# A Fourier layer with a routed expert on one core: second units, the last eight steps and the drain at the end in another order

## The chip, the core and the metric

One core of a Trainium2 chip runs the kernel. Its engines are TensorE (PE in the profile, with PEld for weight loads), VectorE (DVE), ScalarE (ACT), GpSimd (POOL) and SyncE (SP, which here only issues transfers). The metric is the device time of one execution in microseconds (us).

## What is computed

Eight sequences of 3136 rows and 256 columns go through a Fourier layer and then through an expert that sees only the 128 rows of each sequence with the highest scores:

```python
X = np.fft.rfft(x, axis=1)
Yr = Xr @ w_r - Xi @ w_i + b_r
Yi = Xr @ w_i + Xi @ w_r + b_i
Yr, Yi = soft_threshold(Yr, 0.01), soft_threshold(Yi, 0.01)
y = np.fft.irfft(Yr + 1j * Yi, n=3136, axis=1)
scores = y @ w_gate                        # per sequence b:
top = the 128 rows with the highest score
out[top] = y[top] + sigmoid(scores[top]) * (relu(y[top] @ w1) @ w2)   # 1024 hidden
```

## The kernel before

The transform of length 3136 is split into two stages of 98 and 32, so a sequence passes four matmul stages with transfers through DRAM between them:

- `s1` (L398 on, matmul L405) is the first forward stage, eight **units** a sequence; its result is copied by ACT (`at`) and stored in `As`. `fold` (L394) prepares its input.
- `s2` (L439) is the second forward stage, on `As` loaded as `av`; ACT and DVE split its result into `Xh` and `Xl` (L451, L452). `spectral` (L223 to L225, 18 matmuls, called SPEC below) multiplies with the weights; ACT writes `ks`, POOL `kb`, DVE adds it to `py`; `shrink` makes `Y` (ACT L477, DVE L479).
- `s2i` (L500) is the inverse second stage. Its result lies in the left halves of the PSUM tiles `pca` and `pcb`; ACT copies both (`ct`, L510), DVE reads both for the scores (`junk`, L512, which writes `Csc`), and the copies are stored in `Cs`.
- `s1i` (L568) is the inverse first stage, again eight units a sequence, on `Cs` loaded as `cv` (the loads of C; for the last sequence two of them go into the tiles `xt`). Its result goes through ACT (`ot`, L570) to the output.

`s1` and `s1i` share one PSUM tile, `s`. The same tile takes `spread` (L540), a part of the routing.

**The steps.** There are T = 100 steps t, one for each group (13 groups for an even sequence, one of them shared with the next, 12 for an odd one). A step issues on PE, in this order: `s2` of step t + 1; a first unit of `s1` or `s1i`, if one is due; one turn of the routing; SPEC of step t; pieces of the expert; `s2i` of step t - 1; and then a second unit or a `spread`, if one is due. In 18 steps the second unit is one of `s1i`, in one step at the start one of `s1`. Units fall due at 64 in 100 steps, by `due`.

**The routing** of a sequence (`route`) starts when its last `s2i` is done: `score`, `spread`, eight rounds of `select` that find the score of the 128th row digit by digit (PE sums counts at L239, DVE compares and counts again at L234 to L260), then `place`, which makes the row numbers `idx` (PE L281 to L315). Every round puts small results into the right half of `pca`. A routing is a generator with phases "pe", "da" and "db"; `turn` runs one phase of all of them, so that one step makes one round.

**The expert** of a sequence is `fetch` (an indirect transfer by POOL that collects rows from the output, L330) and then `prepare`, `hidden` (L359), `combine` (L370) and an indirect store (L376). `tick` issues one piece of it. `fetch` needs `idx` and all stores of that sequence's output.

**The end.** After the last step, a loop makes slots: one turn of the routing and `work`, which issues pieces of the expert and left-over units of `s1i` until a load estimate is reached. Before the last `s2i` stands `work(3.6)`. The four loads of C of the last sequence (number 7), 784 KB each, are issued when `rest`, the list of units still to do, has shrunk to 8, 8, 6 and 4.

All engines run the order that the program writes (manual schedule). Transfers issue on SP in program order.

Of the kernel before, what the change touches and what calls it, by code (L numbers as in the profile page):

```python
# [104 lines left out]
def fourier_moe(ctx: ExitStack, tc: tile.TileContext, x, w_r, w_i, b_r, b_i, wg, w1, w2,  # L105
# [121 lines left out]
    def select(b, rep, thrs):  # L227
# [3 lines left out]
        for k, i in enumerate(shifts):  # L231
            c = pool.tile([128, S // 8], BF16, name="c", bufs=1)
            n = pool.tile([128, 1], F32, name="n", bufs=1)
            nc.vector.tensor_scalar(out=c, in0=rep, scalar1=f.bitcast(F32), scalar2=None, op0=ALU.is_ge, op1=ALU.add, accum_out=n)  # L234
            if k > 0 and i > 0:
                nc.vector.tensor_tensor(out=g, in0=digits[:, k + 1:k + 2], in1=w, op=ALU.bitwise_xor)  # L236
# [97 lines left out]
    def bank(b, k):  # L334
        return ("m", "s", "m", "px")[k] if b == B - 1 else ("m", "py", "m", "py")[k] if done["t"] >= T else "m"

# [297 lines left out]
    def fetch():  # L634
        for b in range(B):
            for k in range(NCHK):
                while done["s1i"] < b or done["t"] < (40 if b < B - 3 else T - 4) or (b, k) not in slots or len(fetched) > 1:
                    yield
                fetched.append((b, k, slots[b, k], gather(b, k, slots[b, k])))
                age[b, k] = 0  # L640
                yield

    def ffn():
        for e in range(B * NCHK):
            while not fetched or age[fetched[0][:2]] < (6, 0)[fetched[0][0] > B - 3] or done["t"] < T - 2 and fetched[0][0] > B - 4:
                for f in fetched:
                    age[f[:2]] += 1
                yield
            item = fetched[0]
            if item[0] == B - 1:  # L650
                idle(12)
            xT, ga = prepare(*item)
# [9 lines left out]
    def turn(*phases):  # L662
        for phase in phases:
            for g in list(threads):
                if g[1] == phase:
# [9 lines left out]
    def due(u):  # L675
        if 0 <= u < T:
            return [divmod(i, U) for i in range(-(-(u * B * U) // T), -(-((u + 1) * B * U) // T))]
        return []

    def flush():  # L680
# [28 lines left out]
    for t in range(-1, T):  # L709
# [6 lines left out]
        for b, i in due(t - LAG + 3):  # L716
            if b < B - 1:
                ld_c(b, i)
        if t in (0, 4, 8):
# [13 lines left out]
        if t in first:  # L733
            pairs.append((s1, 1, first[t]))
        for _ in due(t - LAG) if t < T else rest[:1]:
            pairs.append((s1i, *rest.pop(0)))
# [20 lines left out]
        if t == T - 1:  # L757
            shrink(*units[t], py, r)
        if 0 <= t - 1 < T:
            b, g = units[t - 1]  # L760
# [10 lines left out]
    def work(us):  # L771
        while load[0] < us:
            was = load[0]
            if rest and turns[0] % 3 == 0 and (rest[0][0] < B - 1 or done["c7"] + 4 < t):
                s1i(*rest.pop(0))
                load[0] += 1.0
                turns[0] += 1
                continue
            tick(ffns)
            turns[0] += 1  # L780
            if load[0] == was and (not rest or turns[0] % 3):
                if not rest or not (rest[0][0] < B - 1 or done["c7"] + 4 < t):
                    break
                turns[0] = 0

    turns = [0]
    while threads or ffns:
        done["t"] = t
        flush()
        for b, i in due(t - LAG + 3):  # L790
            if b < B - 1:
                ld_c(b, i)
        load[0] = 0.0
        if t == T:
            work(3.6)
            s2i(*units[T - 1])
            done["s2i"] = B - 1
            flush()
            load[0] = 0.0
        for k in range(4):  # L800
            if len(rest) <= 8 - 2 * max(0, k - 1) and t > T and (B - 1, k) not in cv:
                ld_c(B - 1, 2 * k)
                ld_c(B - 1, 2 * k + 1)
        turn("pe", "da", "db")
        work(1.0)
        if threads:
            fill(1.0)
        t += 1
# [27 lines left out]
```

## Time and profile before

| | |
|---|---|
| median of 3 runs | 759.39 us (758.47 to 762.05) |
| profiled execution | 754.9 us |
| its span | 753.1 us |
| PE busy | 657.9 us (87%) |
| DVE busy | 439.2 us (58%) |
| ACT busy | 366.9 us (49%) |
| POOL busy | 293.6 us (39%) |
| DMA | 163.73 MB, mean 217 GB/s |

The busy share of an engine is an average over stages. In the steps PE is busy nearly all the time; from about 660 us on, after the last `s2`, it is not. What counts is therefore what PE waits for in each of the two parts.

### The profile page before, as it was taken

Reading aid. Unit: us, or ns where it says so; the run is one execution under the profiler, and the core shown is the slowest. Engines: PE = TensorE matmul, PEld = TensorE weight load, DVE = VectorE, ACT = ScalarE, POOL = GpSimd, SP = SyncE. Lnnn points to the kernel's source line nnn. Section 1 sums busy time; section 2 is a strip of 40 time slices with the busy share of each in tenths; the row PEclk is TensorE's granted clock in tenths of the full one; section 3 lists DMA queues with packets and bytes.
Section 4 is the critical chain, followed back from the end, with each engine's and each line's share of the span. In section 5 each row is a group of like instructions: output and inputs, shape, how many; then the busy total and the mean of one; then the engine's idle time right before and its main releaser. Section 6 shows DMA issues by size and latency. Waiting matters only on the chain.

```text
span 753.1 us, 20432 instructions
## 1 busy us (share of the span) xinstructions
PE 657.9 (87%) x8338; PEld 482.3 (64%) x8338; DVE 439.2 (58%) x1389; ACT 366.9 (49%) x671; POOL 293.6 (39%) x247
## 2 busy tenths in 40 slices
PE   3779989999999899999998999899989999976764
PEld 1347767677766677676676677667667677754534
DVE  4525575776677556566567546655676568744310
ACT  1335555565655556545545555554554455441220
POOL 4247545545435445435345345345431132311001
PEclk9879999999999999999999999999999999998877
DMA  8989777999999989969398678969684657547350
GB/s 161 297 200 351 200 209 205 257 270 261 271 239 288 297 248 270 294 181 282 106 253 258 208 206 252 294 165 266 195 238 141 163 184 225 155 117 209 95 169 15
DMA packets 79198, 163.73 MB, mean 217 GB/s; under 512 B 5918, under 2 KB 58496, under 8 KB 72832
## 3 DMA queue, kind: packets, MB, share of 16 engines
q1 hardware_dynamic: 77920, 160.15, 74.9%
q0 software_dynamic: 896, 2.17, 1.0%
q8 instruction: 66, 1.08, 0.6%
q14 instruction: 28, 0.23, 0.1%
q10 hardware_dynamic: 288, 0.10, 0.1%
HBM read 84.35 MB, written 78.12 MB: 216 GB/s over the span
## 4 chain that ended last, share of the span: by engine, by line
PE 56%; DMA 15%; DVE 12%; ACT 7%; issue 5%; SPq 2%; POOL 2%; POOLq 0%; DVEq 0%; ACTq 0%
PE pca L500 11%; PE s L405 5%; PE px L439 4%; PE py L223 4%; PE py L224 4%; PE py L225 4%; PE pcb L223 3%; PE s L568 3%; PE m L359 3%; DVE junk L512 3%; DMA xt<-in_x 3%; ACT ot L570 2%; ACT ct L510 2%; PE m L370 2%; DMA cv<-Cs 2%
## 5 line engine op out<-in xcount | busy, mean ns | idle before, releaser
L468 POOL TENSOR_TENSOR kb<-ks,bias 128x512 f32<-128x512 f32 x100 | 128.0, 1280 | 342.4 <-ACT ks L466 330.6
L510 ACT COPY ct<-pcb 128x256 f32<-128x256 f32 (+1 forms) x100 | 37.2, 372 | 224.4 <-PE pcb L500 215.4
L394 POOL TENSOR_TENSOR sd<-xt 113x512 f32<-113x512 f32 x106 | 133.9, 1284 | 27.1 <-DMA xt<-in_x 10.8
L472 DVE TENSOR_TENSOR py<-py,kb 128x512 f32<-128x512 f32 x100 | 69.9, 699 | 92.0 <-POOL kb L468 85.7
L452 DVE TENSOR_TENSOR Xl<-px,Xh 128x768 fp32r<-128x768 f32 x100 | 95.6, 956 | 38.9 <-ACT Xh L451 38.9
L500 PE MATMUL pca<-Y,gi_sb 64*64 64x256 f32 x760 | 102.7, 389 | 5.0 <-DVE pca L236 3.9
L500 PE MATMUL pcb<-Y,gi_sb 64*64 64x256 f32 x768 | 103.8, 389 | 0.0
L439 PEld LDWEIGHTS px<-g_sb,av 64*64 64x64 f32 x3072 | 77.9, 135 | 27.1 <-issue 16.1
L512 DVE CUSTOM_DVE_ANT_0 junk<-pcb,wgb 128x256 f32<-128x256 f32 (+1 forms) x100 | 42.3, 423 | 85.8 <-ACT ct L510 84.7
L405 PE MATMUL s<-sd,w 49*64 49x512 f32 x480 | 70.1, 624 | 25.4 <-ACT ot L570 13.1
L451 ACT CAST Xh<-px 128x768 fp32r<-128x768 f32 x100 | 81.2, 812 | 17.1 <-PE px L439 15.7
L439 PE MATMUL px<-g_sb,av 64*64 64x96 f32 x3072 | 84.1, 246 | 5.3 <-DMA av<-As 5.1
L477 ACT ACTIVATE r<-py,m2l 128x512 f32<-128x512 f32 x100 | 70.1, 701 | 6.8 <-DVE py L472 6.8
L407 ACT COPY at<-s 128x1024 f32<-128x1024 f32 x58 | 59.9, 1034 | 24.8 <-PE s L405 24.7
L568 PE MATMUL s<-cv,wi_sb 64*64 64x512 f32 x464 | 61.9, 603 | 9.0 <-DMA cv<-Cs 6.3
L479 DVE SCALAR_TENSOR_TENSOR Y<-py,r 128x512 f32<-128x512 f32 x100 | 68.5, 685 | 1.6 <-ACT r L477 1.6
L500 PEld LDWEIGHTS pca<-Y,gi_sb 64*64 64x64 f32 x760 | 45.0, 132 | 34.7 <-DVE pca L236 8.9
L223 PE MATMUL pcb<-wsh,Xh 128*128 128x256 f32 x200 | 65.5, 328 | 0.9 <-DVE Csc L512 0.9
L570 ACT COPY ot<-s 128x1024 f32<-128x1024 f32 x58 | 59.9, 1033 | 12.6 <-PE s L568 11.9
L223 PE MATMUL py<-wnh,Xh 128*128 128x256 f32 x200 | 57.0, 285 | 1.1 <-DVE Y L479 0.9
L225 PE MATMUL pcb<-wsl,Xh 128*128 128x256 f32 x200 | 56.4, 282 | 0.0
L224 PE MATMUL pcb<-wsh,Xl 128*128 128x256 f32 x200 | 56.4, 282 | 0.0
(169 smaller groups left out, 1364.9 us busy)
## 6 DMA issues: line engine op xcount, KB each, us to landing
Cs<-ct SPq DMA_DIRECT2D x48, 512.0 KB
av<-As SPq DMA_DIRECT2D x46, 512.0 KB
As<-at SPq DMA_DIRECT2D x30, 784.0 KB
cv<-Cs SPq DMA_DIRECT2D x30, 784.0 KB
out<-ot SPq DMA_DIRECT2D x60, 384.0 KB
xt<-in_x SPq DMA_DIRECT2D x56, 384.0 KB
cv<-in_x SPq DMA_DIRECT2D x8, 384.0 KB
As<-ot SPq DMA_DIRECT2D x2, 784.0 KB
```

Of the source, the lines that this page charges most:

```text
L223: nc.tensor.matmul(out, wh, mh, start=start, stop=False)
L224: nc.tensor.matmul(out, wl, mh, start=False, stop=False)
L225: return nc.tensor.matmul(out, wh, ml, start=False, stop=stop).ins
L394: eng.tensor_tensor(out=f[:113, k], in0=t[:113, 0], in1=t[:113, 1], op=op)
L405: nc.tensor.matmul(p[64 * c:64 * c + 64, r, :], w[64 * r:64 * r + NH, c, :], f[64 * r:64 * r + NH, c], start=True, stop=True)
L439: nc.tensor.matmul(o[:, :, N2 * j:N2 * j + N2], a[64 * p:64 * p + 64, j, g % 4, 128 * h + 64 * q:128 * h + 64 * q + 64], g_sb[64 * p:64 * ...
L451: nc.scalar.copy(out=vh, in_=v)
L452: nc.vector.tensor_tensor(out=vl, in0=v, in1=vh.bitcast(F32), op=ALU.subtract)
L468: nc.gpsimd.tensor_tensor(out=kb[:r], in0=ks[:r].broadcast_to([r, 2, D]), in1=bias[:r], op=ALU.add)
L500: nc.tensor.matmul(p[q][64 * a:64 * a + 64], gi_sb[64 * q:64 * q + 64, g, c, 64 * a:64 * a + 64], y[64 * q:64 * q + 64, c, :], start=(c == ...
L568: nc.tensor.matmul(p[64 * c:64 * c + 64, r, :], wi_sb[64 * r:64 + NH * r], f[64 * r:64 + NH * r, 4 * c + 2 * e:4 * c + 2 * e + 2, :], star ...
L570: nc.scalar.copy(out=t[:, :, e, :], in_=p)
```

## The change

1. The second unit (or the `spread`) of a step is issued ahead of `s2i` and no longer behind it.
2. A table `plan` replaces `due` for `s1i`: in each of the last eight steps one unit of sequence 6 is done, so that all eight are done within the steps. Before, five of them were, and three stood behind the last SPEC. `loads` issues the loads of C three steps ahead, in the last eight steps two.
3. The steps 97, 98 and 99 end with a second `turn` of the routing, behind `s2i`.
4. At the end, `work(0.8, True)`, two pieces of the expert and no units, stands ahead of the last `s2i` in the place of `work(3.6)`. All four loads of C of sequence 7 are issued directly behind the store of the last `s2i`. Its units start at slot T + 5, one a slot. The routing of sequence 7 goes ahead of that of 6 on PE.
5. In `select`, the update of the word `w` is moved behind the next count `c` of a round, where it is followed by `g` as before.
6. The expert starts by step numbers (`age`) in place of counted ticks; 6 in place of 12 idle matmuls stand ahead of the last expert.

```diff
+            if k > 1:
+                nc.vector.scalar_tensor_tensor(out=w, in0=d, scalar=shifts[k - 1], in1=w, ...)
+            elif k > 0:
+                nc.vector.tensor_copy(scores[:, b, :], p)
...
-            while not fetched or age[fetched[0][:2]] < (6, 0)[fetched[0][0] > B - 3] or ...
+            while not fetched or done["t"] < age[fetched[0][:2]] or ...
...
+            for g in list(threads) if done["t"] < T else list(threads)[::-1]:
...
+    plan = [due(t - LAG) if t < T - 8 else [] for t in range(T)]
+    for k, v in enumerate([(b, i) for b in range(B - 1) for i in range(U)][sum(map(len, plan)):]):
+        plan[T - 8 + k].append(v)
...
+            loads[t - 3 if t < T - 8 else t - 2].append(v)
...
+        if spreads and not pairs:
+            spreads.pop(0)()
+        pair()
         if 0 <= t - 1 < T:
             b, g = units[t - 1]
             s2i(b, g)
...
-        if spreads and not pairs:
-            spreads.pop(0)()
-        pair()
+        if t > T - 4:
+            turn("pe", "da", "db")
...
-            work(3.6)
+            work(0.8, True)
             s2i(*units[T - 1])
...
-            if len(rest) <= 8 - 2 * max(0, k - 1) and t > T and (B - 1, k) not in cv:
+            if t >= T and len(rest) <= (16, 16, 10, 8)[k] and (B - 1, k) not in cv:
                 ld_c(B - 1, 2 * k)
                 ld_c(B - 1, 2 * k + 1)
...
-        work(1.0)
+        us = 0.8 if t == T else 1.4 if t == T + 1 else 1.2 if t < T + 10 else 0.8
+        work(us, t < T + 2)
```

The lines of the changed kernel are two to ten higher: L500 is L502 there, L568 is L570, L405 is L407, L439 is L441, L239 is L243, L281 is L283.

On PE, in a step with a second unit (step 34 of before; `pcb` and `pca` are `s2i`, `s` the units). Before:

```order
L225 MATMUL py<-wdl,Xh 128x256
L500 MATMUL pca<-Y,gi_sb 64x256 x2
L500 MATMUL pcb<-Y,gi_sb 64x256 x2
L500 MATMUL pca<-Y,gi_sb 64x256 x2
L500 MATMUL pcb<-Y,gi_sb 64x256 x2
L568 MATMUL s<-cv_85,wi_sb 64x512 x4
L439 MATMUL px<-g_sb,av 64x3x32 x16
L405 MATMUL s<-sd,w 64x512 x4
L239 MATMUL pca<-digits,n 128x15
```

And the same place now:

```order
L225 MATMUL py<-wdl,Xh 128x256
L570 MATMUL s<-cv_85,wi_sb 64x512 x4
L502 MATMUL pca<-Y,gi_sb 64x256 x2
L502 MATMUL pcb<-Y,gi_sb 64x256 x2
L502 MATMUL pca<-Y,gi_sb 64x256 x2
L502 MATMUL pcb<-Y,gi_sb 64x256 x2
L441 MATMUL px<-g_sb,av 64x3x32 x16
L407 MATMUL s<-sd,w 64x512 x4
L243 MATMUL pca<-digits,n 128x15
```

The second unit has moved from behind `s2i` to between SPEC and `s2i`; between it and the next user of the tile `s` there now stand `s2i` and `s2`.

On PE, at the passage from step 97 to step 98 (from `s2i` of step 97 to SPEC of step 98). Before:

```order
L500 MATMUL pca<-Y,gi_sb 64x256 x2
L500 MATMUL pcb<-Y,gi_sb 64x256 x2
L439 MATMUL px<-g_sb,av 64x3x32 x16
L239 MATMUL pca<-digits,n 128x15
L223 MATMUL pcb<-wsh,Xh 128x256
```

And now, where `mask` and `tm` belong to `place` of sequence 6:

```order
L502 MATMUL pca<-Y,gi_sb 64x256 x2
L502 MATMUL pcb<-Y,gi_sb 64x256 x2
L243 MATMUL pca<-digits,n 128x15
L441 MATMUL px<-g_sb,av 64x3x32 x16
L570 MATMUL s<-cv_85,wi_sb 64x512 x4
L283 LDWEIGHTS mask
L283 MATMUL pca<-tm,mask 64x98
L223 MATMUL pcb<-wsh,Xh 128x256
```

The last round of the selection has moved from behind `s2` to directly behind `s2i`, a unit has come in, and `place` has begun one step earlier. Step 98 ends in the same way, with the second matmul of `place` (L289) directly behind `s2i`.

On SP, the issues of the end (`Cs7` is C of sequence 7, `out_6` and `out_7` the outputs of sequences 6 and 7). Before:

```order
L523 DMA Cs7_77<-ct_8937 64x8x256 x2
L155 DMA out_6<-ot_9111 96x1x1024 x2
L155 DMA out_6<-ot_9111 2x2x1024
L155 DMA xt0_82<-Cs7_77 98x2048
L155 DMA xt1_83<-Cs7_77 98x2048
L155 DMA out_7<-at_9314 96x1x1024 x2
L155 DMA out_7<-at_9314 2x2x1024
L155 DMA cv0_84<-Cs7_77 98x2048
L155 DMA out_7<-at_9364 96x1x1024 x2
L155 DMA out_7<-at_9364 2x2x1024
L155 DMA cv1_85<-Cs7_77 98x2048
```

And now:

```order
L155 DMA out_6<-ot_9010 96x1x1024 x2
L155 DMA out_6<-ot_9010 2x2x1024
L525 DMA Cs7_77<-ct_8954 64x8x256 x2
L155 DMA xt0_82<-Cs7_77 98x2048
L155 DMA xt1_83<-Cs7_77 98x2048
L155 DMA cv0_84<-Cs7_77 98x2048
L155 DMA cv1_85<-Cs7_77 98x2048
L155 DMA out_7<-at_9311 96x1x1024 x2
```

The last store of sequence 6 has moved ahead of the last store of C, and all four loads follow that store without an output store between them.

On PE behind the last `s2i` there now stand, in this order: four pieces of `hidden` (8 matmuls), `score` of sequence 7, the last four matmuls of `place` of sequence 6, two of `combine`, `spread`, four of `combine`, and the first round of the selection of sequence 7. On ACT the relu that the four pieces of `hidden` need stands behind the four `ct` copies of the last two `s2i`.

## Rows read from the trace of the kernel before

**Rows 1.** Waits of PE: waiter, releaser, us in total, times, longest.

```profile
PE s L405 <- ACT ot L570: 13.1, 15, 1.5
PE m L341 <- DMA xe<-out,idx: 12.6, 2, 8.9
...
PE s L568 <- DMA cv<-Cs: 6.3, 1, 6.3
...
PE s L568 <- ACT ot L570: 2.7, 4, 0.7
```

**Rows 2.** Windows: length, busy PE, PEld, DVE, ACT, POOL, granted clock, DMA share, GB/s.

```profile
125.00:275.00 150.00, 141.03 (x2006) 103.09 (x2003) 102.84 (x335) 87.37 (x162) 72.22 (x58) 1.00 0.95 264
275.00:550.00 275.00, 255.79 (x3343) 190.72 (x3335) 166.47 (x545) 147.12 (x269) 119.58 (x97) 0.99 0.79 228
```

**Rows 3.** PE timeline over a step with a second unit: start, us, what [idle before].

```profile
233.90 0.36 PE L223 MATMUL pcb<-wsh,Xh 128*128 128x256 f32 x1
...
237.34 1.04 PE L568 MATMUL s<-cv,wi_sb 64*64 64x512 f32 x8
238.20 0.84 PE L439 MATMUL px<-g_sb,av 64*64 64x96 f32 x32
239.87 1.09 PE L405 MATMUL s<-sd,w 49*64 49x512 f32 x8 [0.83 <-ACT ot L570]
...
241.14 0.36 PE L223 MATMUL pcb<-wsh,Xh 128*128 128x256 f32 x1
...
246.30 0.36 PE L223 MATMUL pcb<-wsh,Xh 128*128 128x256 f32 x1
```

**Rows 4.** PE timeline of a late step without a unit, and the next.

```profile
641.77 0.43 PE L500 MATMUL pca<-Y,gi_sb 64*64 64x256 f32 x2 [0.18 <-DVE pca L236]
...
642.68 0.84 PE L439 MATMUL px<-g_sb,av 64*64 64x96 f32 x32
644.40 0.40 PE L239 MATMUL pca<-digits,n 128*128 128x15 f32 x2 [0.87 <-DVE Csc L512]
...
649.80 0.39 PE L239 MATMUL pca<-digits,n 128*128 128x15 f32 x2
```

**Rows 5.** ACT timeline of the step of rows 3.

```profile
237.59 0.37 ACT L510 COPY ct<-pcb 128x256 f32<-128x256 f32 x1 [2.29 <-PE pcb L500]
```

**Rows 6.** PE timeline from the last SPEC to the first round of sequence 7.

```profile
667.91 0.38 PE L223 MATMUL pcb<-wsh,Xh 128*128 128x256 f32 x1
...
677.08 0.43 PE L500 MATMUL px<-Y,gi_sb 64*64 64x256 f32 x2
...
685.14 0.29 PE L239 MATMUL pca<-digits,n 128*128 128x15 f32 x2
```

**Rows 7.** DVE timeline: the `Y` that the last `s2i` reads.

```profile
672.24 0.69 DVE L479 SCALAR_TENSOR_TENSOR Y<-py,r 128x512 f32<-128x512 f32 x1 [0.81 <-ACT r L477]
```

**Rows 8.** PE timeline of the slots with rounds of sequence 7.

```profile
697.59 2.93 PE L359 MATMUL py<-xT,w1s 128*128 128x128 f32 x12 [0.28 <-DVE xT L344]
...
703.39 1.14 PE L359 MATMUL m<-xT,w1s 128*128 128x128 f32 x8
704.46 1.09 PE L568 MATMUL px<-xt,wi_sb 64*64 64x512 f32 x8
```

**Rows 9.** SP timeline: the issue of the third load of C of sequence 7.

```profile
709.49 1.17 SPq L155 DMA_DIRECT2D cv<-Cs  x1
```

**Rows 10.** Chain of waits, two gathers of the end: start, us, what.

```profile
690.32 5.96 DMA xe<-out,idx
...
735.51 2.77 DMA xe<-out,idx
```

**Rows 11.** ACT timeline: the copy of the last unit of the program.

```profile
725.71 1.02 ACT L570 COPY ot<-px 128x1024 f32<-128x1024 f32 x1
```

**Rows 12.** Windows of 3 us at the end, columns as in rows 2.

```profile
696.00:699.00 3.00, 2.31 (x10) 2.23 (x11) 1.78 (x8) 0.20 (x1) 0.00 (x0) 0.50 0.00 0
702.00:705.00 3.00, 3.00 (x28) 1.61 (x27) 1.44 (x10) 1.46 (x2) 0.00 (x0) 1.00 0.01 3
```

More of the change, by code (lines that the diff above doesn't have):

```diff
@@ L234, in select @@
             nc.vector.tensor_scalar(out=c, in0=rep, scalar1=f.bitcast(F32), scalar2=None, op0=ALU.is_ge, op1=ALU.add, accum_out=n)
+            if k > 1:
+                nc.vector.scalar_tensor_tensor(out=w, in0=d, scalar=shifts[k - 1], in1=w, op0=ALU.logical_shift_left, op1=ALU.bitwise_xor)
+            elif k > 0:
+                nc.vector.tensor_copy(scores[:, b, :], p)
             if k > 0 and i > 0:
@@ L644, in ffn @@
         for e in range(B * NCHK):
-            while not fetched or age[fetched[0][:2]] < (6, 0)[fetched[0][0] > B - 3] or done["t"] < T - 2 and fetched[0][0] > B - 4:
-                for f in fetched:
-                    age[f[:2]] += 1
+            while not fetched or done["t"] < age[fetched[0][:2]] or done["t"] < T - 2 and fetched[0][0] > B - 4:
                 yield
@@ L650, in ffn @@
             if item[0] == B - 1:
-                idle(12)
+                idle(6)
             xT, ga = prepare(*item)
@@ L663, in turn @@
         for phase in phases:
-            for g in list(threads):
+            for g in list(threads) if done["t"] < T else list(threads)[::-1]:
                 if g[1] == phase:
@@ L678, in due @@
         return []
+    plan = [due(t - LAG) if t < T - 8 else [] for t in range(T)]
+    for k, v in enumerate([(b, i) for b in range(B - 1) for i in range(U)][sum(map(len, plan)):]):
+        plan[T - 8 + k].append(v)
+    loads = [[] for t in range(T)]
+    for t in range(T):
+        for v in plan[t]:
+            loads[t - 3 if t < T - 8 else t - 2].append(v)
     def flush():
@@ L715, in fourier_moe @@
                 ld_a(*units[u])
-        for b, i in due(t - LAG + 3):
-            if b < B - 1:
-                ld_c(b, i)
+        for b, i in loads[t] if t >= 0 else ():
+            ld_c(b, i)
         if t in (0, 4, 8):
@@ L734, in fourier_moe @@
             pairs.append((s1, 1, first[t]))
-        for _ in due(t - LAG) if t < T else rest[:1]:
+        for _ in plan[t] if t >= 0 else ():
             pairs.append((s1i, *rest.pop(0)))
@@ L765, in fourier_moe, with ready, work @@
             shrink(*units[t], py, r)
-        if spreads and not pairs:
-            spreads.pop(0)()
-        pair()
+        if t > T - 4:
+            turn("pe", "da", "db")
     t = T
-    def work(us):
+    def ready():
+        b, i = rest[0]
+        return b < B - 1 or t > T + 4 + 3 * (i // 2) // 2
+    def work(us, alone=False):
+        turns = 0
         while load[0] < us:
             was = load[0]
-            if rest and turns[0] % 3 == 0 and (rest[0][0] < B - 1 or done["c7"] + 4 < t):
+            if not alone and rest and turns % 3 == 0 and ready():
                 s1i(*rest.pop(0))
                 load[0] += 1.0
[L777 to L786, printed above, removed]
+            elif turns % 3 or alone or not rest:
+                tick(ffns)
+            turns += 1
+            if load[0] == was and turns > 6:
+                break
     while threads or ffns:
@@ L799, in fourier_moe @@
             load[0] = 0.0
+            work(1.4)
         for k in range(4):
-            if len(rest) <= 8 - 2 * max(0, k - 1) and t > T and (B - 1, k) not in cv:
+            if t >= T and len(rest) <= (16, 16, 10, 8)[k] and (B - 1, k) not in cv:
                 ld_c(B - 1, 2 * k)
                 ld_c(B - 1, 2 * k + 1)
+        load[0] = 0.0
         turn("pe", "da", "db")
-        work(1.0)
+        us = 0.8 if t == T else 1.4 if t == T + 1 else 1.2 if t < T + 10 else 0.8
+        work(us, t < T + 2)
         if threads:
-            fill(1.0)
+            fill(min(us, 1.0))
         t += 1
```

9 lines of the change are left out of this document (2 added, 7 removed).

## The prediction

> **What bounds the kernel now.** I read the whole-span list of waits for PE first, then the windows, then timelines of single steps, and the end last. The list [rows 1] has four lines that matter here. Two say that a unit waits for the ACT copy of the unit before it: 13.1 us in 15 waits and 2.7 us in 4, nearly all of 0.7 to 0.8 us. Two are single long waits, for a gather (12.6 us in two) and for a load of C (6.3 us in one); they stand in the end. The windows [rows 2] show PE busy for 141 of 150 us and 256 of 275 us at a granted clock of 1.00 and 0.99, so the steps are bound by PE, and what they can give back is PE's own waiting. The end is not bound by an engine: it is a chain of selection rounds, loads, units and stores.
>
> A step with one unit takes 5.40 us, from one L239 to the next, and so does the step without a unit before it, where PE waits 0.87 us [rows 4]. In that step L239 starts 2.63 us after the first matmul of `s2i`: it waits until DVE has read `s2i`'s result. So two limits lie at 5.40: PE's work with one unit, and the loop SPEC, `s2i`, `ct`, `junk`, L239, SPEC.
>
> A step with a second unit goes from SPEC to SPEC in 7.24 us, the next one in 5.16 [rows 3]. Together that is 12.40 against 10.80 for two plain steps, 1.60 more. The unit itself takes 0.86 (from 237.34 to the next matmul, L439, at 238.20), and the first unit of the next step waits 0.83 for the tile `s`, which ACT is still emptying.
>
> **Part 1: the second unit ahead of `s2i`.** Its ACT copy now runs while PE does `s2i` and `s2`, so the 0.83 us go. ACT has room there: it sat idle 2.29 us ahead of the first `ct` [rows 5]. The 0.18 us that `s2i` waits for DVE [rows 4] lie under the unit too. What is left of 1.60 is 0.86 - 0.18 = 0.68, a gain of 0.92 in each of 18 steps, 16.6. The waits in rows 1 give 13.1 + 2.7 = 15.8, of which under 1 us lies in the end. I take 15 as the full gain. What comes next is the loop: SPEC, unit, `s2i`, 2.63, L239. It gives 5.40 + 0.86 - 0.18 = 6.08, the same as PE's work, so there is nothing further to win, and if ACT is late by a few tenths they cost at once. Cover that may run out: up to 275 us the DMA share is 0.95, later 0.79 [rows 2]. Seven of the 18 steps lie in the first stretch, where a shorter step asks for more than the engines have shown. I take 1 us off: **14**, between 0 (the wait only moves) and 16.6. The six spreads that move along I count as 0: no wait in rows 1 names one.
>
> **Part 2: three units into steps without one.** A step without a unit and one with a unit both take 5.40 [rows 4], so they cost 0 where they come. If the cover (the loop) were gone, it would be 3 x 1.04 = 3 us.
>
> **Part 3: the second turn in steps 97 to 99.** Here the change adds a wait. In step 97 a round, in step 98 a matmul of `place`, stands directly behind `s2i` and writes `pca`. It can start 2.63 us after `s2i`'s start, and PE needs 0.91 for `s2i` (L500 to L439) [rows 4], so PE stands still for 1.72, twice; `s2` and all behind it are queued there. Against that the later wait of 0.87 goes, twice, and one unit (1.04) comes into step 98. 2 x 1.72 - 2 x 0.87 + 1.04 is +2.7, **say 3**. In step 99 the turn has nothing for PE. The sum by this trace rests on L239 having to wait for readers of other columns of the same tile. The Trainium skill, in PSUM — Partial Sum Buffer, section PSUM bank collisions raise a hardware error, says to guard PSUM by bank and quadrant and not by address; by that rule the wait stays whatever the columns are, and the 0.87 us in rows 4 agree. If it went by address, part 3 would cost about 1 and not 3.
>
> **Parts 4 and 2: the end.** I count from S, the start of the last SPEC: 667.91 before [rows 6], with the span's end at S + 85.2.
>
> - The last `s2i` started at S + 9.2 [rows 6], behind two units and the expert's pieces of `work(3.6)`. Its input `Y` was there at 672.93, S + 5.0 [rows 7]. Now only two pieces stand ahead: S + 5.1.
> - (Here and in the rounds, small pieces without a group are means of the trace's groups by line: relu 0.6, copies 0.4 and 0.6, `score` 0.2, `spread` 1.1 to 2.) The first round of the selection of sequence 7 stood at 685.14, S + 17.2 [rows 6]. Now, from S + 5.1: `s2i` to S + 6.2, its copies to S + 7.1, then the relu (0.6), for which four pieces of `hidden` wait; these end at S + 10.1, `score` and four matmuls of `place` at S + 11.2, two of `combine` and `spread` (1.1 to 2) at S + 13, the copy and the count (1.2), with four of `combine` between: S + 15. Bounds: S + 12.5, if the relu isn't late, to S + 17.
> - Rounds. The first takes 2.6, an estimate: a plain one's 1.9 and four small DVE operations. In the next slot `prepare` needs the gather of sequence 6: issued near S + 12.4, it lands 2.8 to 6.0 later [rows 10], by S + 18.4, and PE comes there at S + 18. With xT (1.3) and three pieces: 3.7. Then a slot with three pieces, 2.0. Then five slots of a round, a unit and a piece: 0.25 to 0.39 for the round's matmul [rows 4], 1.09, and half of 1.14 [rows 8], 1.9 each. The last round, three slots of `place` and the units 5 to 8 between them: 1.9 + 1.3 + 1.3 + 1.1. From S + 15 that is S + 36.6 for the last unit and S + 37.7 for its copy.
> - The loads of C. The third was issued only at 709.49 [rows 9], behind output stores, and its unit waited 6.3 us [rows 1]. Now all four stand behind the store of C, near S + 12.5. At the 264 GB/s of rows 2, 3.2 MB take 12.2 us: all there at about S + 25, and the four are needed from S + 23, 27, 31 and 34 on. No wait.
> - From the last copy (its end at 726.73 [rows 11]) to the gather at 735.51 [rows 10] were 8.8 us of stores, and from there 17.6 to the end of the span. I leave both. So the end is S + 37.7 + 8.8 + 17.6 = S + 64.1, against 85.2: **-21**, between -16 (slots of 2.2, gather late) and -25.
>
> **Parts 5 and 6** count as 0. `g` closes the same run of DVE instructions as before and L239 waits for it; were PE waiting for the count alone, eight rounds would give 8 x 0.2 = 1.6. The expert's work is the same, only at other steps.
>
> **Sum.** -14 + 3 - 21 = -32. The profiled execution, 754.9 us with a span of 753.1, becomes 722.9 with 721.1. It lies 4.5 us below the median of the runs shown, so the median becomes 759.4 - 32 = **727.4**.
>
> **Rivals.**
>
> - *The wait moves (0.12).* The moved unit's copy (1.05) now stands on ACT ahead of `ct`, and `ct` is in the loop. If ACT comes to it late, `ct`, `junk` and L239 are late by what was won. For it: the loop and PE's work tie at 6.08. Against it: ACT's 2.29 us of idle time in rows 5. Part 1 gives 0: 741.
> - *The DMA engines are the bound (0.13).* In the first 275 us the share is at 0.95; seven steps keep their time (+6), and at the end the gather of sequence 6 shares the engines with 3.2 MB of C and lands only behind them, at S + 25, which holds the second round for 7. 727.4 + 13 = 740. For it: the 5.96 us of the gather in rows 10, with two loads in flight. Against it: no wait of PE for a transfer in rows 1 lies in the steps.
> - *The clock stays up (0.08).* In the end TensorE was granted 0.50 (1.2 GHz) in the window 696 to 699, after a wait of PE, and 1.00 (2.4 GHz) in 702 to 705 [rows 12]; twelve rows of `hidden` took 2.93 us at the one, eight took 1.14 at the other [rows 8], so 1.2 us more. If the shorter waits leave the clock at 2.4 GHz, `spread`, `hidden` and a unit give some 4 us: 723. The Trainium skill (TensorE: Matmul & The Clock Gate, Part 1) says that an idle PE drops to half rate; the window agrees, but that the new waits are short enough no row shows.
> - *Slower (0.04).* The clock falls inside the steps: PE stands still for 1.7 us twice at the end, and the steps become denser. At half rate, by 2.93 against 1.71 us for twelve rows, a step of 5.40 takes 9.2, 3.8 more. Nine such steps eat the gain, ten make it slower by 0.5%: 765 with ten. Against it: 0.99 to 1.00 in 425 us of steps [rows 2].
>
> **How the numbers follow.** The forecast has 0.63: 719 to 735. The four rivals have the rest. Faster by over 0.5% (3.8 us, about what a measurement of this kernel can tell from no change) is the forecast and the first three, less a little for both of the first two at once with something unseen: 0.93; within it 0.03; slower 0.04. The range takes in the two rivals at 740: 717 to 741.
>
> **What would show it.** Right: the line of L407 waiting for ACT `ot` is gone or under 2 us; SPEC to SPEC is 6.1 in a step with a second unit and 5.4 in the next; PE idles 1.7 us before L243 and before L289 at the ends of steps 97 and 98; the four loads of C are issued in a row and no unit waits for them; the last SPEC comes about 11 us earlier, and the end 64 us behind it. Wrong: waits of PE for `ct` or Csc in the steps with a second unit, a line of waits for DMA in the steps, or a second round that waits for the gather.

## The result, and the profile after

The changed kernel takes 732.5 us (median of four runs, 729.4 to 733.1), the kernel before took 758.9 beside it (756.4 to 762.1). The ratio is 0.964, with an interval from 0.960 to 0.969: 26 us less, where 32 were forecast. The profiled execution took 729.4, with a span of 727.5 (before: 753.1). Some executions of a kernel were over 1.5% longer than its fastest, at a lower granted clock of TensorE; the ratios leave them out, and the profiles of e0 and e11 are of such executions.

To see where the time went I cut both spans at the same instructions, the first matmul of SPEC (L223) of certain steps. Column a-b runs from the SPEC of step a to that of step b (the difference of the two start times, in us), the last column from the start S of the last SPEC, 99, to the end of the span. The other rows are kernels of the next section.

| kernel | first SPEC | 0-11 | 11-35 | 35-37 | 37-67 | 67-70 | 70-96 | 96-99 | end |
|---|---|---|---|---|---|---|---|---|---|
| before | 50.5 | 57.0 | 138.8 | 14.0 | 207.0 | 19.9 | 162.9 | 17.9 | 85.2 |
| after | 52.5 | 57.4 | 134.8 | 12.8 | 197.6 | 20.5 | 161.5 | 21.7 | 68.7 |
| e0_after_again | 52.2 | 60.1 | 134.7 | 19.4 | 197.2 | 23.2 | 160.7 | 21.7 | 68.6 |
| e1_unit_first_alone | 51.8 | 57.4 | 135.2 | 15.7 | 196.6 | 18.8 | 159.7 | 17.9 | 85.8 |
| e2_unit_last_again | 51.1 | 57.8 | 141.2 | 13.4 | 207.0 | 20.8 | 165.4 | 21.7 | 69.1 |
| e3_select_back | 51.1 | 57.3 | 133.0 | 18.1 | 196.7 | 21.1 | 159.8 | 22.9 | 66.5 |
| e4_no_late_turns | 52.8 | 57.4 | 135.9 | 15.1 | 197.0 | 22.0 | 161.5 | 18.7 | 61.0 |
| e9_w2_later | 52.7 | 57.2 | 135.7 | 11.0 | 196.9 | 20.5 | 161.6 | 21.7 | 69.2 |
| e8_combined | 52.5 | 57.2 | 133.0 | 17.7 | 200.1 | 23.0 | 160.5 | 18.4 | 58.0 |
| e10_combined_w2_later | 52.5 | 58.9 | 133.8 | 11.0 | 197.0 | 20.7 | 160.6 | 18.4 | 57.8 |

So the gain stands in two places, the steps with a second unit (11 to 35 and 37 to 67) and the end, and 3.9 us are lost in 96-99. The last SPEC came 9.1 us earlier, where about 11 were forecast.

The list of PE's waits (waiter, releaser, us in total, times, longest) no longer has the two lines of [rows 1] for ACT `ot`, nor a wait of a unit for `cv`. What stands ahead now, besides one wait of 10.7 us at the start that was there before too:

```profile
PE m L343 <- DMA xe<-out,idx: 11.5, 4, 8.3
...
PE pca L502 <- DVE pca L240: 5.5, 19, 0.3
```

A step with a second unit on PE, the step of [rows 3] and the one behind it (start, us, what):

```profile
233.32 0.37 PE L223 MATMUL pcb<-wsh,Xh 128*128 128x256 f32 x1
...
235.62 1.09 PE L570 MATMUL s<-cv,wi_sb 64*64 64x512 f32 x8
236.53 0.38 PE L502 MATMUL pca<-Y,gi_sb 64*64 64x256 f32 x2
...
238.05 1.04 PE L407 MATMUL s<-sd,w 49*64 49x512 f32 x8
239.16 0.39 PE L243 MATMUL pca<-digits,n 128*128 128x15 f32 x2
239.40 0.36 PE L223 MATMUL pcb<-wsh,Xh 128*128 128x256 f32 x1
...
244.75 0.37 PE L223 MATMUL pcb<-wsh,Xh 128*128 128x256 f32 x1
```

SPEC to SPEC is 6.08 us where it was 7.24, with no wait of PE left in it, and the step behind takes 5.35 where it took 5.16.

A step with one unit and a round, the kind of [rows 4]:

```profile
626.04 0.37 PE L223 MATMUL pcb<-wsh,Xh 128*128 128x256 f32 x1
...
628.70 0.43 PE L502 MATMUL pca<-Y,gi_sb 64*64 64x256 f32 x2 [0.28 <-DVE pca L240]
...
631.58 0.36 PE L223 MATMUL pcb<-wsh,Xh 128*128 128x256 f32 x1
```

It takes 5.54 instead of 5.40 us, and `s2i` waits 0.28 us for `g` where it waited 0.18. That is a loss in steps that I had held unchanged.

The end on PE, with the rows that answer to [rows 6], [rows 8] and the last expert's:

```profile
663.90 0.65 PE L502 MATMUL px<-Y,gi_sb 64*64 64x256 f32 x4 [0.59 <-DVE Y L481]
...
666.57 2.05 PE L361 MATMUL m<-xT,w1s 128*128 128x128 f32 x16 [1.25 <-ACT hh L366]
...
674.59 0.29 PE L243 MATMUL pca<-digits,n 128*128 128x15 f32 x2
...
679.51 0.41 PE L343 MATMUL m<-ident,xe 128*128 128x128 f32 x2 [1.93 <-DMA xe<-out,idx]
680.44 2.48 PE L361 MATMUL py<-xT,w1s 128*128 128x128 f32 x12 [0.52 <-DVE xT L346]
682.71 0.45 PE L243 MATMUL pca<-digits,n 128*128 128x15 f32 x2
...
697.25 1.09 PE L570 MATMUL px<-cv,wi_sb 64*64 64x512 f32 x8
...
711.31 0.69 PE L343 MATMUL m<-ident,xe 128*128 128x128 f32 x2 [8.33 <-DMA xe<-out,idx]
712.61 3.75 PE L361 MATMUL s<-xT,w1s 128*128 128x128 f32 x16 [0.61 <-DVE xT L346]
716.15 3.08 PE L361 MATMUL m<-xT,w1s 128*128 128x128 f32 x16
719.07 3.62 PE L372 MATMUL px<-w2s,hh 128*128 128x256 f32 x16
```

From S = 658.85 the last `s2i` starts at S + 5.05 and the first round of sequence 7 at S + 15.7. The third, which stands behind the gather of sequence 6, comes only at S + 23.9, where S + 21.3 follows from the forecast's slots. In the chain of waits that gather is the longest transfer behind S; it runs while the four loads of C are under way, whose issues stand in a row on SP:

```profile
671.61 7.76 DMA xe<-out,idx
```

```profile
671.00 0.75 SPq L155 DMA_DIRECT2D xt<-Cs  x2
671.84 1.09 SPq L155 DMA_DIRECT2D cv<-Cs  x2
```

And the windows of the two expert passages (length, busy PE, PEld, DVE, ACT, POOL, granted clock, DMA share, GB/s) show TensorE at the lower of its two levels, 1.2 GHz, behind both waits for a gather:

```profile
681.00:684.00 3.00, 3.00 (x17) 3.00 (x16) 0.70 (x4) 0.00 (x0) 0.00 (x0) 0.50 0.82 298
...
714.00:717.00 3.00, 3.00 (x16) 3.00 (x15) 0.00 (x0) 0.54 (x1) 0.00 (x0) 0.50 0.03 5
```

### The profile page after: what moved, and what is told of

It is laid out like the page before. It is cut to its first block, busy times and chain, and to the rows that moved or that the text cites. A ratio compares the mean times of both kernels' runs of the same rounds, so it can differ in the third digit from the quotient of the medians.

```text
span 727.5 us, 20428 instructions
## 1 busy us (share of the span) xinstructions
PE 650.9 (89%) x8333; PEld 479.8 (66%) x8333; DVE 443.8 (61%) x1393; ACT 364.6 (50%) x671; POOL 293.5 (40%) x247
## 4 chain that ended last, share of the span: by engine, by line
PE 59%; DVE 14%; DMA 12%; issue 6%; ACT 6%; POOL 2%; SPq 1%; POOLq 0%; DVEq 0%; ACTq 0%
PE pca L502 9%; PE s L570 6%; PE px L441 5%; DVE junk L514 5%; PE py L223 5%; PE py L225 4%; PE py L224 4%; PE s L407 4%; PE pcb L223 4%; PE m L361 3%; PE m L372 3%; DVE Xl L454 2%; ACT ct L512 2%; PE pcb L225 2%; PE pcb L224 2%
## 5 line engine op out<-in xcount | busy, mean ns | idle before, releaser
L396 POOL TENSOR_TENSOR sd<-xt 113x512 f32<-113x512 f32 x106 | 133.8, 1284 | 28.4 <-DMA xt<-in_x 20.3
L512 ACT COPY ct<-pcb 128x256 f32<-128x256 f32 (+1 forms) x100 | 37.3, 373 | 170.5 <-PE pcb L502 159.8
L502 PE MATMUL pca<-Y,gi_sb 64*64 64x256 f32 x760 | 101.8, 386 | 5.8 <-DVE pca L240 5.5
L502 PE MATMUL pcb<-Y,gi_sb 64*64 64x256 f32 x768 | 103.3, 386 | 0.0
L441 PEld LDWEIGHTS px<-g_sb,av 64*64 64x64 f32 x3072 | 78.9, 135 | 19.2 <-issue 5.7
L441 PE MATMUL px<-g_sb,av 64*64 64x96 f32 x3072 | 84.3, 246 | 5.5 <-DMA av<-As 5.3
L407 PE MATMUL s<-sd,w 49*64 49x512 f32 x480 | 72.7, 638 | 12.9 <-DVE sd L396 10.7
L572 ACT COPY ot<-s 128x1024 f32<-128x1024 f32 x58 | 60.1, 1036 | 44.8 <-PE s L570 44.8
L502 PEld LDWEIGHTS pca<-Y,gi_sb 64*64 64x64 f32 x760 | 46.5, 132 | 41.9 <-issue 11.3
L223 PE MATMUL pcb<-wsh,Xh 128*128 128x256 f32 x200 | 65.7, 328 | 1.2 <-DVE Csc L514 1.2
L570 PE MATMUL s<-cv,wi_sb 64*64 64x512 f32 x464 | 62.6, 599 | 0.0
L223 PE MATMUL py<-wnh,Xh 128*128 128x256 f32 x200 | 56.8, 284 | 1.3 <-DVE Y L481 1.2
```

The source lines that it names most:

```text
L223: nc.tensor.matmul(out, wh, mh, start=start, stop=False)
L396: eng.tensor_tensor(out=f[:113, k], in0=t[:113, 0], in1=t[:113, 1], op=op)
L407: nc.tensor.matmul(p[64 * c:64 * c + 64, r, :], w[64 * r:64 * r + NH, c, :], f[64 * r:64 * r + NH, c], start=True, stop=True)
L441: nc.tensor.matmul(o[:, :, N2 * j:N2 * j + N2], a[64 * p:64 * p + 64, j, g % 4, 128 * h + 64 * q:128 * h + 64 * q + 64], g_sb[64 * p:64 * ...
L502: nc.tensor.matmul(p[q][64 * a:64 * a + 64], gi_sb[64 * q:64 * q + 64, g, c, 64 * a:64 * a + 64], y[64 * q:64 * q + 64, c, :], start=(c == ...
L570: nc.tensor.matmul(p[64 * c:64 * c + 64, r, :], wi_sb[64 * r:64 + NH * r], f[64 * r:64 + NH * r, 4 * c + 2 * e:4 * c + 2 * e + 2, :], star ...
```

## The experiments

**The changed kernel again** (e0_after_again).

> The changed kernel itself, once more, beside the three runs that it is to be compared with. Expected: 732.5 us again, 731 to 734, and the same trace: last SPEC near 659, the gather of sequence 6 landing 7 to 8 us after its issue while four loads of C are under way, PE's wait for it 1.9 us. A second trace also tells whether that long gather repeats: if it was chance, it lands within 3 to 4 us here and PE doesn't wait.

733.2 us (728.0 to 739.9), ratio 0.965 (0.962 to 0.969). The gather of 6 landed 8.4 us after its issue, so the long gather repeats. PE waited 0.9 us for it here, for the first round came later too, at S + 18.6; the third round stood at S + 25.7 and the span ended at S + 68.6. Where the two traces of this kernel part is told in the last section.

**Part 1 alone** (e1_unit_first_alone), the kernel before with

```diff
+        if spreads and not pairs:
+            spreads.pop(0)()
+        pair()
         if 0 <= t - 1 < T:
             b, g = units[t - 1]
             s2i(b, g)
             ...
-        if spreads and not pairs:
-            spreads.pop(0)()
-        pair()
```

> Kernel before with part 1 alone: the second unit (and the spread) ahead of s2i, nothing else. Theory (the copy of the unit now runs beside s2i and s2): the waits of L405 for ACT ot, 13.1 us in 15, are gone; SPEC to SPEC is 6.08 instead of 7.24 in a step with a second unit; 14 to 17 us off, 759 - 15.5 = 743.5. Rival (the wait only moves to ct on ACT): steps of 7.0 to 7.2 and 757 to 759. In between, with the transfers of the first 275 us as the bound: 749.

740.2 us, ratio 0.976 (0.972 to 0.979) over a before of 758.4: 18.2 less. The waits of L405 for ACT `ot` shrank from 13.1 us in 15 to one of 0.4:

```profile
PE s L405 <- ACT ot L570: 0.4, 1, 0.4
```

The step of [rows 3] takes 6.07, and the step behind it stays at 5.17 (239.25 to 244.42 here); I had expected that one to grow to 5.40, as it does behind two other steps with a second unit (19 and 29). The end is what it was (85.8). So part 1 is worth more than its "full" gain, and neither the ACT rival nor the value in between holds for the whole.

**Part 1 undone** (e2_unit_last_again): the same lines moved back in the changed kernel.

> The changed kernel with part 1 undone: the second unit behind s2i again. There are eight more steps with one unit less to place than before, so 15 steps have a second unit. Theory: the waits for ACT ot are back, 12 to 14 us, and the time is 732.5 + 12 to 16 = 746. Rival (the gain in the steps comes from where the FFN pieces and units of the last eight steps now stand, and not from the place of the second unit): within 2 us of 732.5.

750.4 us, ratio 0.990 (0.987 to 0.994): 17.9 more than the changed kernel, and the waits are back:

```profile
PE s L407 <- ACT ot L572: 12.5, 15, 0.9
```

From both sides part 1 is worth 17 to 18 us. All the rest of the change together is worth about 8 of the 26. The end is 69.1 here, as in the changed kernel, so what the end gained is of the other parts; parts 2, 4 and 6 were not run alone.

**Part 5 undone** (e3_select_back):

```diff
-            if k > 1:
-                nc.vector.scalar_tensor_tensor(out=w, in0=d, scalar=shifts[k - 1], in1=w, ...)
-            elif k > 0:
-                nc.vector.tensor_copy(scores[:, b, :], p)
...
                 nc.vector.tensor_tensor(out=f, in0=digits[:, 1:2], in1=w, op=ALU.bitwise_xor)
+                nc.vector.tensor_copy(scores[:, b, :], p)
             elif i > 0:
                 nc.vector.scalar_tensor_tensor(out=f, in0=d, scalar=i, in1=g, ...)
+                nc.vector.scalar_tensor_tensor(out=w, in0=d, scalar=i, in1=w, ...)
```

> The changed kernel with part 5 undone: w is again computed behind f, in the round's last group, and not between the count c and g. Theory (g stands behind w in DVE's row, so L243's matmul and with it s2i's first matmul come 0.13 later in a step with a round): the wait of s2i for DVE g falls from 0.31 to 0.17 us, the single-unit steps with a round from 5.54 to 5.41, and some 30 such steps give 3 to 4 us: 729. In the eight rounds of the end nothing or 0.1 each. Rival (w costs as much where it stood, between f and the next count): within 1 us of 732.5.

730.6 us, ratio 0.964 (0.961 to 0.967): by the time alone not to be told from the changed kernel. The steps tell it: those with one unit and a round take 5.41 again, and over steps 12 to 97 the differences of 0.12 to 0.23 us sum to 3.0 in 21 steps. The expected 30 steps were too many. DVE's rows of one round say why (changed kernel, then this one):

```profile
622.01 0.15 DVE L262 SCALAR_TENSOR_TENSOR f<-d,pca 128x1 uint32<-128x1 uint32 x1
622.21 0.62 DVE L234 TENSOR_SCALAR_CACHE_REDUCE c<-rep,f 128x392 bf16<-128x392 f32 x1
622.75 0.08 DVE L234 DVE_READ_ACCUMULATOR c<-rep,f 128x1 f32 x1
622.75 0.16 DVE L236 SCALAR_TENSOR_TENSOR pca<-d,pca 128x1 uint32<-128x1 uint32 x1
622.94 0.16 DVE L240 TENSOR_TENSOR pca<-digits,pca 128x1 uint32<-128x1 uint32 x1
```

```profile
622.36 0.15 DVE L259 SCALAR_TENSOR_TENSOR f<-d,pca 128x1 uint32<-128x1 uint32 x1
622.55 0.17 DVE L260 SCALAR_TENSOR_TENSOR pca<-d,pca 128x1 uint32<-128x1 uint32 x1
622.62 0.61 DVE L234 TENSOR_SCALAR_CACHE_REDUCE c<-rep,f 128x392 bf16<-128x392 f32 x1
623.16 0.08 DVE L234 DVE_READ_ACCUMULATOR c<-rep,f 128x1 f32 x1
623.16 0.16 DVE L236 TENSOR_TENSOR pca<-digits,pca 128x1 uint32<-128x1 uint32 x1
```

Behind `c`, `w` (L236 in the first) puts 0.19 us ahead of `g`, which reads it; between `f` and `c` (L260 in the second) it costs 0.07, since `c` doesn't read it and starts 0.07 later. From `f` to the end of `g` that is 1.09 against 0.96 us, the 0.13 by which the step is longer. These rows are no full rule: `w` in the second starts 0.19 behind `f`, though it doesn't read it.

**Part 3 undone** (e4_no_late_turns):

```diff
-        if t > T - 4:
-            turn("pe", "da", "db")
```

> The changed kernel with part 3 undone: no second turn behind s2i in steps 97 to 99, so a round and place of sequence 6 stand one phase later, and with them the gather of sequence 6, which now comes behind the second round of sequence 7. Theory (part 3 costs 3.7 us of steps, and the gather that it brings forward falls among the loads of C, so it wins nothing back): steps 97 and 98 take 5.2 and 7.3 us instead of 7.34 and 8.86, the last SPEC comes 3.7 us earlier, no round waits for the gather, and the end behind the last SPEC is as long as before or up to 2 us shorter: 727 to 729. Rival (part 3 is needed, since the rounds of 7 or the pieces of the expert of 6 come later without it): the end grows by 3.7 or more and the time is 732.5 or above.

723.3 us, ratio 0.953 (0.950 to 0.957): 9 us less than the changed kernel, about twice what the theory expected. The steps give back 3.0 us (18.7 against 21.7 in 96-99). The end shrinks by 7.7, from 68.7 to 61.0, where at most 2 were expected. On PE the third round now stands at S + 21.2, S being 660.39:

```profile
675.43 0.29 PE L243 MATMUL pca<-digits,n 128*128 128x15 f32 x2
...
681.56 0.39 PE L243 MATMUL pca<-digits,n 128*128 128x15 f32 x2 [1.00 <-DVE pca L240]
...
687.12 0.44 PE L343 MATMUL m<-ident,xe 128*128 128x128 f32 x2
...
694.94 1.09 PE L570 MATMUL px<-cv,wi_sb 64*64 64x512 f32 x8
```

The expert of 6 (L343) comes behind the fifth round here, not ahead of the third, and the last unit starts at S + 34.6 instead of S + 38.4.

**Only the expert later** (e11_expert_later) keeps part 3 and changes one number:

```diff
-                age[b, k] = done["t"] + (2 if b < B - 2 else 3 if b < B - 1 else 0)
+                age[b, k] = done["t"] + (2 if b < B - 2 else 6 if b < B - 1 else 0)
```

> The changed kernel with the expert of sequence 6 begun six slots behind its gather instead of three; part 3 stays. On PE the rounds, units and pieces behind the second round of sequence 7 then stand in the same order as in the kernel without the late turns. Theory (that kernel's end was 7.6 us shorter because no round of 7 has the expert of 6 ahead of it, nor waits for its gather): the third round stands at 20 to 21.5 us behind the last SPEC instead of 23.9, the last unit's copy 36 to 37 behind it instead of 40.6, the end 61 to 63 instead of 68.65; the steps keep part 3's 3.7 us: 726. Rival (the shorter end comes from what part 3 moves in steps 97 to 99): the end stays at 66 to 69 us and the time at 731 or above.

729.6 us with a wide spread (725.2 to 736.8); the ratio, 0.957 (0.953 to 0.961), stands for 726.4. In the profiled execution TensorE was granted only 0.69 on the mean from S + 9 to S + 18, and the first round came at S + 19.0, so the end (65.2) can't be compared from S. From the first round on it can: 46.3 us to the end of the span, as in e4 (46.0), against 52.9 in the changed kernel, with the last unit 18.0 behind the first round (e4: 19.5, changed kernel: 22.7). The seven traces with part 3 and the expert ahead of the third round take 47.5 to 52.9 for this. The time agrees: 726.4 is 6.1 less than the changed kernel took, and the 3.0 that part 3 costs in the steps lead on to the 723.3 of e4. So most of the 7.7 us is the expert's place among the rounds. The steps keep part 3's loss.

**Idle matmuls up to the last gather** (e6_idle36), `idle(36)` for `idle(6)`.

> The changed kernel with 36 idle matmuls instead of 6 ahead of the last expert, 9 us of PE work in place of the 8.3 us wait for the last gather. Theory (PE stands still so long that TensorE is granted 0.50, and the last expert's hidden runs at that): the granted clock is 1.00 from 701 to the end, hidden takes twice 1.8 us instead of 3.54 and 2.92 from row to row, the two transposes 0.3 less, and the time falls by 3 us: 729.5. Rival (the clock falls there whatever PE does, or idle matmuls hold the transposes back): 732.5 or above.

732.0 us, ratio 0.966 (0.962 to 0.969). The clock stayed at 1.00 and `hidden` took 2.0 us each, as expected:

```profile
717.89 2.02 PE L361 MATMUL s<-xT,w1s 128*128 128x128 f32 x16 [0.61 <-DVE xT L346]
719.75 1.95 PE L361 MATMUL m<-xT,w1s 128*128 128x128 f32 x16
```

The row behind the two passages starts 3.65 us after the first of them, where it was 6.46 in the changed kernel (712.61 to 719.07) and 5.27 in e0: 1.6 to 2.8 gained at this place, and an end of 65.7. The whole time doesn't show it: 35-37 took 16.8 in this profile and 96-99 took 23.3.

**The loads of C behind the gather** (e7_loads_behind_gather): the loads taken out of the loop, and

```diff
             xT, ga = prepare(*item)
+            if item[0] == B - 2:
+                for k, v in enumerate(xts + cvs):
+                    nc.vector.memset(v[32:33, 0, :1], 0.0)
+                    ld_c(B - 1, 2 * k)
```

> The changed kernel with the four loads of C of sequence 7 issued only behind the landing of the gather of sequence 6 (one element of each target is written by DVE first, behind the copy that reads the gather, which the load has to wait for). Theory (the gather took 7.8 us because it shared the DMA engines with 3.2 MB of C): it lands 2.8 to 3.5 us after its issue, PE doesn't wait for it (0.7 for DVE at most), the third round stands 2 us earlier, and the loads, 7 us later, still land before their units: 730.5. Rival (the gather is slow by itself, or waits for the last stores of sequence 6): 6 to 8 us again, and the loads come too late: 733 to 737.

733.9 us (730.1 to 737.5), ratio 0.965 (0.961 to 0.970): no difference in the time. The gather of 6, issued 10 us ahead of the first of the loads (690.46), landed 2.7 us after its issue:

```profile
L332 POOL DMA_INDIRECT xe<-out,idx x1: 981/981/981, 680.4 to 680.4; - x1
...
DMA to landing us min/median/max: 2.7/2.7/2.7
```

In the changed kernel and in the six others that issue it beside the loads of C it took 7.8 to 8.5 us, so the loads made it slow. PE's wait for it is gone, but PE then waited for the copy `xT` on DVE, which was at work on the round:

```profile
688.08 0.44 PE L343 MATMUL m<-ident,xe 128*128 128x128 f32 x2
689.99 1.99 PE L361 MATMUL py<-xT,w1s 128*128 128x128 f32 x12 [1.47 <-DVE xT L346]
...
695.83 1.09 PE L570 MATMUL s<-xt,wi_sb 64*64 64x512 f32 x8 [0.92 <-DMA xt<-Cs]
```

The third round stood at S + 25.2 and the first unit waited 0.9 for its load. From the first round to the end of the span it took 50.6 us, between the two traces of the changed kernel (52.9, and 50.0 in e0). So a faster gather whose price is later loads doesn't shorten the end.

**A combined version** (e8_combined): e3 and e4 together, `idle(12)`, and the units of 7 earlier:

```diff
-        return b < B - 1 or t > T + 4 + 3 * (i // 2) // 2
+        return b < B - 1 or t > T + 2 + i // 2
```

> The changed kernel with what the earlier runs point to: w behind f again (3 us less in the steps), no second turn in steps 97 to 99 (3.7 less), the units of sequence 7 from the second round on, two in a slot while their expert waits (they were held back to the fourth), and 12 idle matmuls. Theory (the end is then bound by the rounds and place of sequence 7 and no longer by its units' stores: last SPEC at 652, the last idx at 39 us behind it, the last gather landing at 43, the end at 57 to 60): 712 to 718. Rival (the stores or the loads of C set the end as before, the units wait for C): 65 us behind the last SPEC, 722 to 726.

716.6 us, ratio 0.942 (0.939 to 0.945). The end took 58.0, in the range expected, with the last unit at S + 27.7. The last SPEC was expected at 652 and came at 662.3: 35-37 took 17.7 us, and the step from SPEC 42 to 43 took 10.9 instead of 7.4, 2.6 of it a wait for a gather. Where the former go, PE and the windows show:

```profile
248.00 0.54 PE L447 MATMUL px<-gt_sb,at 64*64 64x192 f32 x4 [1.97 <-DMA at<-As]
249.44 0.92 PE L447 MATMUL px<-gt_sb,at 64*64 64x192 f32 x10 [0.90 <-DMA at<-As]
```

```profile
245.00:250.00 5.00, 2.14 (x33) 1.21 (x36) 2.17 (x6) 1.24 (x3) 2.87 (x3) 0.98 1.07 337
250.00:255.00 5.00, 5.00 (x28) 3.15 (x21) 1.21 (x2) 2.19 (x3) 0.29 (x1) 0.50 1.00 250
```

PE waits 2.9 us for loads of `at` while the DMA engines are full, and then works at 1.2 GHz through the 5 us of the second row.

**Less to load there** (e9_w2_later, the changed kernel; e10_combined_w2_later, the combined one):

```diff
-        if t in (24, 28, 32, 36):
-            consts_moe((t - 24) // 4)
+        if t in (24, 28, 40, 44):
+            consts_moe((24, 28, 40, 44).index(t))
```

> The changed kernel with the two loads of w2 (0.5 MB each), which the expert needs only from step 44 on, issued in steps 40 and 44 instead of 32 and 36. Theory (up to 262 us the DMA engines are the bound, so what part 1 wins in the steps before is given back in steps 36 and 37, where PE waits 1 to 3.4 us for the load of at, and in most profiles TensorE is granted 0.50 behind that wait): the wait for at falls by the 1.8 us that 0.5 MB take, to 0 to 1.5 us, steps 36 and 37 take 13 us instead of 12.8 to 19.4, and the time is 728 to 730. Rival (the loads of A wait for their stores, not for room on the engines): steps 36 and 37 as in the other runs, 15 to 19 us, and 732.5.

> The combined kernel (w behind f, no second turn in steps 97 to 99, units of sequence 7 from the second round on, 12 idle matmuls) with the loads of w2 in steps 40 and 44. Theory: 716.6 less 3 to 5 us, 712 to 714, steps 36 and 37 at 13 us instead of 17.7. Rival (the wait comes back at the next load, or at the gather of step 43): 716.6.

e9: 729.0 us, ratio 0.960 (0.956 to 0.964), 3.5 less than the changed kernel, though the two intervals overlap. The trace is clearer: the wait for `at` is gone, and the stretch 35-37 (the expectations number its steps by their ends, 36 and 37) takes 11.0 us, less than the 13 expected. e10: 714.9 us (712.1 to 720.6), ratio 0.942 (0.937 to 0.946), the fastest here; 35-37 took 11.0 in its profile too, but the gain over e8 is too small to tell by the time.

## Why the prediction was right, and where its terms were off

The forecast was 727.4, in a range of 717 to 741; 732.5 came. Part 1, the two stops of part 3 and the shorter end came by the mechanisms that I named; what part 3 does to the end and what part 5 costs I had wrong. That the total is off by only 5 is in part luck, since errors of both signs cancel: by the times of e1, e2 and e4 part 1 gave 3 to 4 us more than its term and part 3 took 6 more.

- **Part 1, -14.** The waits that I named went, and SPEC to SPEC became 6.08 as worked out. The term was too small: 17 to 18 by e1 and e2. The gain of a pair was right: in e1's trace the 18 steps with a second unit are 17.5 us shorter, and the steps behind them grow by 0.5 in all (two of them to 5.41; the others, as that of [rows 3], stay), which leaves 17.0 where 18 x 0.92 gave 16.6. The step that failed is the rounding down to 15, and the spreads "as 0": the seven steps with a spread are 3.5 us shorter in all, 1.9 of it in step 40, which the kernel before ran at a mean clock of 0.78. Some 4 are given back in the steps 11, 31, 32 and 35, so about 16.5 stand between steps 11 and 96.
- **Its cover.** I took 1 us off for DMA engines near their limit up to 275 us and made the rest a rival of 0.13. The rival holds in part. With part 1 and the loads of w2 in their old place, eight of nine traces wait 1.9 to 3.5 us for `at` in step 35 and take 15.1 to 19.4 us in 35-37, against 14.0 before; the profile of the changed kernel, with 1.1 us of such a wait, was a lucky one. e9 and e10 show the cause by taking 0.5 MB of loads out of the stretch ahead: 11.0 in both. The rival's other half came in part as well: the gather of 6 was slow because of the loads of C (e7), and held the third round, not the second, for 1.9 us.
- **Part 3, +3.** The two stops were 1.53 us each, where 1.72 was worked out, at L243 and L289 as named, and the steps lost 3.0 to 3.9. The Trainium skill (PSUM — Partial Sum Buffer, section PSUM bank collisions raise a hardware error) says to guard PSUM by bank and quadrant, or simply by bank, and not by address. The trace agrees in that the matmul stands 1.53 us for readers of other columns; that the chip would need this wait no run here shows. But the part costs 9 us (e4), not 3. What I missed is what it moves: the gather of 6 comes earlier (issued at S + 12.8, in e4 at S + 20.6), and with it an expert that nobody waits for yet. Its transposes and first pieces stand ahead of the third round, whose chain sets the end, and the units come behind that. I had put those pieces into the slots as work that fills them, 3.7 us for the slot with `prepare`; it took 5.5.
- **The end, -21.** It was -16.5: 68.7 us behind S instead of 64.1. (The slots as I listed them add up to S + 38.4, since the last round's 1.9 stands beside five slots that already hold it; without it they give S + 36.5, and I went on from S + 36.6.) The first round came 0.7 late (S + 15.7 for S + 15), the third 2.6 (S + 23.9 for S + 21.3), with 1.9 of waiting for a gather that I let land "by S + 18.4" and `hidden` at the lower clock, and the copy of the last unit 2.9 (S + 40.6 for S + 37.7). From there to the gather of 7 it was 9.0 us, as left unchanged (8.8). The last stage took 19.1 instead of 17.6: I left it unchanged, but here the second half of `hidden` ran at the lower clock too (2.9 us from its first row to the next row, 1.8 before). The edit from 12 to 6 idle matmuls doesn't explain this: with 12, e1 shows 2.9 as well, and with 6, e0, e3 and e7 show 1.8. e6 bounds what the clock takes there, 2.8 us against this profile. No unit waited for the loads of C, as worked out; what they cost is the slow gather.
- **Part 5, 0.** This was wrong. I wrote that `g` closes the same run of DVE instructions and that L239 waits for it. It is `s2i` that waits for it (19 waits, 5.5 us in all), and `w` costs 0.19 us ahead of `g`, which reads it, where it cost 0.07 ahead of `c`. Over 21 steps the differences sum to 3.0.
- **The rivals.** "The wait moves" is refuted by e1. "The clock stays up" didn't come: both expert passages of the end ran at 0.50. "Slower", by falls of the clock within the steps, came in single steps (below), never in nine. Two of the signs of being wrong came in single steps as well: step 68, which has a second unit, waits 1.4 us for Csc, and steps 42 and 69 wait 0.7 and 0.6 for a gather.

In the profiled execution the terms are then: steps by part 1 about -16.5 (from e1), part 3 in the steps +3.9, part 5 +3.0, the end -16.5, the start of the kernel +2.4 (first SPEC and steps 0 to 11), together -23.7 of -25.6; the remaining -1.9 is less than 35-37 varies by.

## What to carry to other kernels

When an edit brings a piece of work forward, ask which chain it now stands ahead of on its engine, not only what wait it adds: an expert that is due only at the end has its place behind the rounds that everything waits for. Cost a one-row move on DVE from the starts of the rows at its new place (here 0.19 us ahead of a row that reads the result, 0.07 ahead of one that doesn't), and multiply by all the steps in which someone waits for the last row of that run. When a step becomes shorter, look for the place where the transfers catch up with it, and move loads that aren't yet needed out of the stretch ahead of it.

## What the runs showed of the hardware

The same stop of PE had two outcomes. In the changed kernel PE stood for 1.53 us before L243 in step 97, and in e3 for 1.54; the windows behind them:

```profile
647.82 0.39 PE L243 MATMUL pca<-digits,n 128*128 128x15 f32 x2 [1.53 <-DVE Csc L514]
```

```profile
648.00:651.00 3.00, 3.00 (x51) 2.11 (x52) 2.35 (x10) 1.81 (x2) 0.00 (x0) 1.00 0.46 131
```

```profile
647.40 0.39 PE L239 MATMUL pca<-digits,n 128*128 128x15 f32 x2 [1.54 <-DVE Csc L512]
```

```profile
648.00:651.00 3.00, 3.00 (x41) 1.39 (x37) 1.69 (x8) 0.80 (x1) 0.00 (x0) 0.50 0.39 115
```

At 1.00 the step took 7.33 us, at 0.50 it took 8.66. Of the eight traces with part 3, which all have this stop, five took 7.33 to 7.34 us and three 8.66 to 8.92. So a stop of 1.5 us cost 1.5 us in one execution and 2.8 in another. The Trainium skill (TensorE: Matmul & The Clock Gate, Part 1) says that how many matmuls run at the lower clock at a kernel's start varies between runs of one kernel. The two stops shown are in the middle of a run, of two kernels that differ in part 5 alone, and show such a spread there too.

Places of this kind, in 35-37, 67-70, 96-99 and in the end, are where the traces part. In step 35 the changed kernel took 6.85 us at a clock of 1.00 behind a wait of 1.1 us, and 11.06 at a mean of 0.78 behind 3.4 us in e0. In the end, six of the eight traces with part 3 show a mean clock of 0.79 to 0.89 from S + 3 to S + 19 and a first round at S + 17.4 to S + 19.0; the three without part 3 but with the new end (e4, e8, e10) show 1.00 and S + 15.1. Whether the two stops of part 3 bring this about, and what decides it, is not shown here.

An indirect gather of 128 rows landed 2.7 us after its issue in e7, at a DMA share of 0.16, and 7.8 to 8.5 us after it in the seven traces that issue it beside 3.2 MB of loads (0.87 in the changed kernel).
